# Attention with three full heads and a max-out layer: batches 2 and 3 loaded plainly and cast on the engines instead of by casting transfers

## The chip, the core and the metric

The kernel runs on one core of one Trainium2 chip. The metric is the device time of one execution in microseconds (us); lower is better.

## What is computed

```python
scores = q @ k^T / sqrt(64)                      # 4 batches, 8 heads, 768 x 64 each, f32
mask   = causal                                  # for "retrieval" heads (3 of the 8, by a flag array)
       = causal & (key < 4 or query - key < 64)  # for the other heads
a      = softmax(where(mask, scores, -1e9))
x      = (a @ v), heads side by side             # 3072 x 512
out    = maximum(x @ w1, x @ w2) @ w_out         # w1, w2: 512 x 1024; w_out: 1024 x 512
```

The kernel uses max(h1, h2) = relu(h1 - h2) + h2, so it multiplies x by w1 - w2, applies relu to get g, and adds x @ (w2 @ w_out) to g @ w_out. The product w2 @ w_out (`w2o` in the code) is made once.

## The kernel before

The work is cut into eight halves: four batches, each with two halves of 384 query rows. A half has two parts. *Attention* works on four pairs of heads. The heads are sorted at the start by the flags, so that the full heads come first. q and k are needed in bf16 and turned (head dimension on the partitions), v in bf16 as it lies. TensorE makes the scores (line 814), ScalarE the exponentials (833), VectorE applies masks (852) and divides by the sums (894, 904), and TensorE forms the weighted sums of v (877). The result x of a half is turned: by TensorE for batch 0 (1007), by a transposing transfer on SyncE for the others (1026). *Forward* is 32 up matmuls against w1 - w2 (1098), eight relus, and 36 down matmuls (1141) against w_out and w2o, then three copies to SBUF and three stores (1159).

How q, k and v come to bf16 differs by batch. For batches 0 and 1, `load_half` (492) loads f32 on SyncE's queue. The f32 tiles are cast by GpSimd, VectorE or ScalarE (`cast_qk`, `cast_v`), TensorE transposes q and k (`turn`, 655), and VectorE or ScalarE copies the turned tile out of PSUM (`unturn`). For batches 2 and 3, `load_pair` (522) issues casting transfers on GpSimd's queue (533), six for a pair, and one transposing transfer on SyncE's queue (546) turns q and k of a pair. A pair's destination is read from registers that hold the sorted heads.

There are three f32 buffers for loads (`NLD = 3`); A and B (the two halves of batch 0), w2, w1 and then the halves of the other batches take them in turn, and a load waits until the buffer's former tenant has been cast. w_out comes in four quarters as casting transfers on GpSimd's queue (`load_down`, 577, line 579). There are four output buffers (`NOUT = 4`).

The order of all instructions is fixed when the program is built. The class `Order` (`run`, 189) is a planner: each operation has a cost for each engine that can do it, the operations it depends on, and a rank, and the planner walks through planned time, giving each free engine its ready operation of lowest rank. TensorE has eight lists, searched in the order of `PE_LISTS`. Where the planner sees TensorE idle before `WARM_UNTIL`, it writes dummy matmuls on a tile of zeros (`warmer`, 457) into the program. What it writes is a fixed order on every engine, including the order of transfers on SyncE's and GpSimd's queues; on the chip each instruction then waits for its own semaphores, and everything behind it on its engine waits as well.

The lines that choose the way of a batch and the order of the first loads:

```python
LOADS = (
    'A', 'wo1', 'B', 'w22', 'w21', 'w12', 'w20', 'wo0', 'wo2', 'w10', 'masks', 'w11', 'w13',
    'w23', 'wo3',
)
LONG = ((0, 0), (0, 1), (1, 0), (1, 1))   # halves whose q and k come in one transfer, 768 B rows
CAST_BY_DMA = (2, 3)                      # batches that load_pair loads
...
        if b in CAST_BY_DMA:              # in prepare()
            if hf == 0:
                T["pair", n] = load_pair(b, p)
```

Of the kernel before, what the change touches and what calls it, by code (L numbers as in the profile page):

```python
# [12 lines left out]
BF16 = mybir.dt.bfloat16  # L13
I32 = mybir.dt.int32
ALU = mybir.AluOpType
ACT = mybir.ActivationFunctionType
# [119 lines left out]
class Order:  # L136
# [51 lines left out]

    def run(self, names, allowed):
        free = dict.fromkeys(("PE", "ACT", "DVE", "POOL", "SP"), 0.0)  # L190
        free["SP"], free["PE"] = 1.1, PE_BEGINS
        done_pe = []

        def used(t, span=3.4):
# [75 lines left out]
        while events:  # L270
            t = events[0][0]
# [79 lines left out]
        return max(o.end for o in self.ops)  # L351


WARM_UNTIL = 45.0
REGISTERS = 4.4
TURNED_BY_PE = (0,)
CAST_QK = {'POOL': 0.46, 'DVE': 0.27, 'ACT': 0.4}
CAST_V = {'POOL': 0.3, 'DVE': 0.26, 'ACT': 0.26}
RANK = {
    'cast': -1.1, 'vcast': -0.4, 'unturn': 1.2, 'mix_k': -2.6, 'mix_v': -1.1, 'exp': -1.35,  # L360
    'mask': 2.4, 'norm': -1.0, 'take_x': 1.05, 'turn': 1.9, 'w2b': 1.95, 'sub': -0.1, 'w2t':
    -0.75, 'wob': 0.5, 'w2o': -1.7, 'relu': -0.65, 'load': 0.7, 'out': 1.3, 'h2': -2.5,
}
NLD = 3
NQB = 4
# [4 lines left out]
NXT = 4  # L370
NG = 2
NOUT = 4
LONG = ((0, 0), (0, 1), (1, 0), (1, 1))
PE_LISTS = ('TX', 'W', 'S', 'TQ', 'P', 'H', 'P2', 'F')
PLACES = (0, 1, 2, 0, 1, 2, 0, 1, 2, 0, 1, 2)
SECOND_UP = False
LOADS = (
    'A', 'wo1', 'B', 'w22', 'w21', 'w12', 'w20', 'wo0', 'wo2', 'w10', 'masks', 'w11', 'w13',
    'w23', 'wo3',
)  # L380
BIAS = {'DVE': 2.5, 'ACT': 2.5}
BIAS_MIX = {}
W2B_BEHIND = True
NORM = {'DVE': 0.35}
TURNED_BY_DMA = ()
DMA_TURN = 0.19
PACE = 2
W2O_EARLY = 3
X_LAST = ((0, 0),)
BIASED = ((0, 0),)  # L390
DMA_BEGINS = 3.05
CAST_BY_DMA = (2, 3)
CAST_ISSUE = 0.85
CAST_RATE = 0.28
SPARE = {}
STEP = 2.0
FF_STEP = -1.1
S_AFTER = 2
PE_BEGINS = 1.3
COLD_UNTIL = 7.9  # L400
WARM_SHARE = 0.5
SHARE = {'S': 0.7, 'W': 0.9}
MARGIN = {'W': 0.3, 'S': 0, 'TQ': 0, 'F': 0.4}
X_MARGIN = 1.5


def tile_three_full_heads(
    tc, q, k, v, w1, w2, wo, out, tab, table_dram, heads, rez, found, verdict
):

    nc = tc.nc
# [30 lines left out]
    xts = keep.tile([128, NXT, NT, KC, 128], BF16, name="xt")  # L442
    gs = keep.tile([128, NG, FC, HALF], BF16, name="g")
    ots = keep.tile([128, NOUT, d_model], F32, name="ot")
    warm = keep.tile([128, 128], BF16, name="warmer")
    ones = keep.tile([128, 1], BF16, name="ones")
    banks = [psum.tile([128, 512], F32, name=f"ps{e}") for e in range(8)]
    nc.gpsimd.memset(warm, 0.0)  # L448
    nc.vector.memset(ones, 1.0)
    nc.gpsimd.memset(vbs[:, :, :, :, D:VW], 1.0)  # L450

# [70 lines left out]
    def load_pair(b, p):  # L522

        n = b * HP + p
        if p == 0:
            slot_of[b, 0], old, tenants[b] = slot()
            staged_old[b] = old
        got = {}
        for hh in range(2):
            for t, src in enumerate((q, k, v)):  # L530
                def emit(_, t=t, src=src, hh=hh):
                    to = vbs[:, n % NQK, hh, :, 0:D] if t == 2 else staged(n)[:, :, t, hh]
                    nc.gpsimd.dma_start(  # L533
                        out=to,
                        in_=src[b, bass.ds(heads[2 * p + hh], 1)].rearrange("o (i p) d -> p (o i) d", p=128),
                    )
                o = op(
                    {"POOL": CAST_ISSUE}, emit, [registers, *(last_w.get(n - NQK, ()) if t == 2 else ())],
                    data=0.197 / CAST_RATE, rank=RANK["load"], tag=f"load{b}.{p}", port=("POOL",),
                )  # L540
                if t < 2:
                    later.append((o, staged_old[b]))
                got[t, hh] = o

        def turn_pair(_):
            nc.sync.dma_start_transpose(
                out=qks[:, n % NQK].rearrange("f t (i c) -> f (t i) c", c=128),
                in_=staged(n).rearrange("p i t h d -> p (i t h d)"),
            )
        un = op(  # L550
            {"SP": 1.7}, turn_pair, [got[t, hh] for t in range(2) for hh in range(2)] + list(last_s.get(n - NQK, ())),
            data=DMA_TURN * 4 * NT, tag=f"turn{b}.{p}", rank=RANK["turn"],
        )
        tenants[b].append(un)
        return un, [got[2, 0], got[2, 1]]
# [21 lines left out]
    def load_down(c, behind):  # L577
        def emit(_):
            nc.gpsimd.dma_start(
                out=wob[:, 2 * c:2 * c + 2],  # L580
                in_=wo.rearrange("(c p) f -> p c f", p=128)[:, 2 * c:2 * c + 2],
            )
        return op({"POOL": 0.8}, emit, behind, data=2.097 / 4 / 0.36, rank=-1.0, tag=f"wo{c}")

    slot_of, tenants, bias_in, table_in, staged_old = {}, {}, [], [], {}
    w1_in, w2_in, wo_in, flow = {}, {}, {}, []
# [328 lines left out]
    def attend(b, hf):  # L915
# [81 lines left out]
        if b in TURNED_BY_PE:  # L997
            for c, tiles_ in enumerate(((0, 1), (2,))):
                key = ("px", b, hf, c)

                def emit(_, key=key, tiles_=tiles_):
                    px = bank(key, BF16)
                    x = xs[:, (2 * b + hf) % NX].rearrange("p i h d -> p i (h d)")
                    for e, i in enumerate(tiles_):
                        for kc in range(KC):
                            at = (e * KC + kc) * 128
                            nc.tensor.transpose(
                                px[:, at:at + 128], x[:, i, kc * 128:kc * 128 + 128], ident
                            )

                def take(e, key=key, tiles_=tiles_):
                    n = len(tiles_) * KC * 128
                    copy(
                        e, xts[:, (2 * b + hf) % NXT, tiles_[0]:tiles_[0] + len(tiles_)].rearrange("f i k c -> f (i k c)"),
                        bank(key, BF16)[:, 0:n],
                    )
                cols = len(tiles_) * KC * 128
                o = pe("TX", mm(*[128] * (len(tiles_) * KC)), emit, mine, claims=[(key, 1)])
                x_free.setdefault(len(x_free) if c == 0 else len(x_free) - 1, []).append(o)
                ready.append(op(  # L1020
                    {"DVE": 0.03 + cols / 1780, "ACT": act(cols)}, take, [o, *old],
                    frees=[key], rank=RANK["take_x"],
                ))
        else:
            def emit(_):
                nc.sync.dma_start_transpose(
                    out=xts[:, (2 * b + hf) % NXT].rearrange("f i k c -> f (i k) c"),
                    in_=xs[:, (2 * b + hf) % NX].rearrange("p i h d -> p (i h d)"),
                )
            o = op({"SP": 0.5}, emit, [*mine, *old], data=2.2, rank=-1.0)  # L1030
            x_free[len(x_free)] = [o]
            ready.append(o)
        x_ready[b, hf] = ready
# [347 lines left out]
def head_order(nc, small, is_retrieval, H):  # L1381

    raw = small.tile([1, 2 * H], I32, name="raw")
    nc.sync.dma_start(
        out=raw, in_=bass.AP(tensor=_as_int32(is_retrieval, 2 * H), offset=0, ap=[[0, 1], [1, 2 * H]])
    )
    number = small.tile([1, H], F32, name="number")
    for h in range(H):
        nc.vector.memset(number[:, h:h + 1], float(H - h))
    flag = small.tile([1, 2 * H], F32, name="flag")  # L1390
    r = small.tile([1, H], F32, name="r1")
    key = small.tile([1, H], F32, name="key")
    top = small.tile([1, H], F32, name="top")
    found = small.tile([1, H], F32, name="found")
    found_i = small.tile([1, H], I32, name="found_i")
    count = small.tile([1, 1], F32, name="count")
    vec = nc.vector
    vec.tensor_single_scalar(out=flag, in_=raw, scalar=0.0, op=ALU.not_equal)
    two = flag.rearrange("p (h two) -> p h two", two=2)
    vec.tensor_tensor(out=r, in0=two[:, :, 0], in1=two[:, :, 1], op=ALU.max)  # L1400
    vec.scalar_tensor_tensor(
        out=key, in0=r, scalar=2.0 * H, in1=number, op0=ALU.mult, op1=ALU.add
    )
    vec.max(out=top, in_=key)
    vec.tensor_scalar(
        out=key, in0=top, scalar1=2.0 * H, scalar2=-2.0 * H, op0=ALU.is_gt, op1=ALU.mult
    )
    vec.tensor_tensor(out=key, in0=key, in1=top, op=ALU.add)
    vec.tensor_scalar(
        out=found_i, in0=key, scalar1=-1.0, scalar2=float(H), op0=ALU.mult, op1=ALU.add  # L1410
    )
    vec.tensor_reduce(out=count, in_=r, op=ALU.add, axis=AX.X)
    return found_i, count
# [3 lines left out]
def kernel(  # L1417
# [38 lines left out]
    with tc.tile_pool(name="consts", bufs=1) as consts:  # L1456
        tab = consts.tile([128, table.shape[1]], BF16, name="tab")
        warm = consts.tile([128, 1], F32, name="warm")
        rez = consts.tile([128, B * H * S // 128], F32, name="rez")
        verdict = consts.tile([1, 1], I32, name="verdict")  # L1460
        found, count = head_order(nc, consts, is_retrieval, H)
        nc.scalar.dma_start(out=tab[:, 0:128], in_=table_dram.ap()[:, 0:128])
        nc.vector.memset(warm, 0.0)
# [4 lines left out]
        )  # L1468
        tile_three_full_heads(
            tc, q, k, v, moe_w1, moe_w2, moe_w_out, out, tab, table_dram, heads, rez, count,  # L1470
            verdict,
        )
        right = nc.values_load(
            verdict, min_val=0, max_val=1, skip_runtime_bounds_check_because="a product of two flags"
# [43 lines left out]
```

## Time and profile before

| | |
|---|---|
| three runs | 190.79, 192.16, 192.37 us (median 192.16) |
| profiled execution | 192.47 us, of which the profile's span is 190.8 us |
| busy of the span | TensorE 169.0, ScalarE 125.9, VectorE 87.8, GpSimd 58.7 us |
| moved | 32.10 MB in 89616 packets, 72946 of them under 512 bytes |
| mean granted TensorE clock | 0.974 |

The page gives busy times of one execution. PE is TensorE, PEld its weight loads, ACT ScalarE, DVE VectorE, POOL GpSimd, and SP SyncE, which only issues transfers; "SPq" and "POOLq" are issues of transfers. L1141 is line 1141 of the kernel. A group's row gives the count, then busy time and the mean time of one in ns, then the idle time just before and what ended it. In the rows of windows the columns are the stretch, its length, busy time and count of PE, PEld, DVE, ACT and POOL, the granted clock, the mean busy share of the transfer engines and GB/s. In a tile's row, three numbers with slashes are the shortest, the median and the longest in ns.

### The profile page before, as it was taken

How to read it: one execution, taken by the hardware profiler on the slowest of the kernel's cores; microseconds unless marked ns; L12 is line 12 of the kernel's file. 1: busy time of each engine (PE TensorE's matmuls, PEld its weight loads, DVE VectorE, ACT ScalarE, POOL GpSimd, SP SyncE). 2: the span in 40 equal slices, each digit the busy share in tenths (PEclk: the TensorE clock that was granted, in tenths of full speed). 3: DMA queues.
4: the chain of work that ended last, by engine and by line, in shares of the span. 5: the costliest groups of instructions: out<-in, count | busy, mean ns of one | idle time of the engine just before them, and what ended most of it. 6: DMA issues, size and time to landing. Idle time of an engine off the chain costs nothing.

```text
span 190.8 us, 4666 instructions
## 1 busy us (share of the span) xinstructions
PE 169.0 (89%) x1690; PEld 101.2 (53%) x1710; DVE 87.8 (46%) x261; ACT 125.9 (66%) x259; POOL 58.7 (31%) x98
## 2 busy tenths in 40 slices
PE   0999868996699999999999999699999999999960
PEld 0975638564346575566556655356466545445420
DVE  3165987975126668364243663785438500000000
ACT  3179894875448999999866974796978426417220
POOL 1100530357795829965475152000000000000000
PEclk9999985999999999999999999999999999999996
DMA  4999899999999979999999999993411322021121
GB/s 116 348 230 321 211 364 274 372 268 219 185 274 206 133 67 291 164 190 167 187 157 127 213 183 149 149 220 92 123 73 58 75 94 79 5 110 55 53 81 44
DMA packets 89616, 32.10 MB, mean 168 GB/s; under 512 B 72946, under 2 KB 86386, under 8 KB 89586
## 3 DMA queue, kind: packets, MB, share of 16 engines
q1 hardware_dynamic: 50722, 25.92, 59.3%
q0 software_dynamic: 38720, 5.77, 45.2%
q8 instruction: 15, 0.25, 0.5%
q14 instruction: 15, 0.12, 0.2%
q10 hardware_dynamic: 144, 0.03, 0.1%
HBM read 25.69 MB, written 6.29 MB: 168 GB/s over the span
## 4 chain that ended last, share of the span: by engine, by line
PE 64%; DMA 21%; SPq 10%; issue 1%; DVE 0%; ACT 0%; ACTq 0%
PE ps L1141 28%; PE ps L1098 17%; DMA xt<-x 7%; SPq L510 6%; DMA qk<-ld 6%; PE ps L877 6%; PE ps L814 6%; DMA wob<-in_moe_w_out_dram 4%; DMA ld<-in_moe_w_dram 4%; PE ps L1077 4%; SPq L498 2%; PE ps L1059 2%; PE ps L655 1%; SPq L558 1%; SPq L571 1%
## 5 line engine op out<-in xcount | busy, mean ns | idle before, releaser
L833 ACT ACTIVATE at<-ps 128x512 bf16<-128x512 f32 (+2 forms) x134 | 65.1, 569 | 7.6 <-PE ps L814 5.1
L1141 PE MATMUL ps<-wob,g 128*128 128x512 bf16 x184 | 45.8, 379 | 0.6 <-issue 0.3
L1098 PE MATMUL ps<-xt,w 128*128 128x384 bf16 x256 | 45.8, 326 | 0.3 <-DMA xt<-x 0.3
L1122 ACT ACTIVATE g<-ps 128x384 bf16<-128x384 f32 x56 | 27.4, 496 | 7.7 <-PE ps L1098 7.1
L1098 PEld LDWEIGHTS <-w 128*128 128x128 bf16 x256 | 23.5, 98 | 15.3 <-DMA xt<-x 0.8
L852 DVE TENSOR_TENSOR at<-at,tab 128x1024 bf16<-128x1024 bf16 (+5 forms) x49 | 24.0, 513 | 8.1 <-ACT at L833 7.8
L466 ACT COPY ot<-ps 128x512 f32<-128x512 f32 x21 | 12.3, 588 | 22.8 <-PE ps L1141 22.6
L1141 PEld LDWEIGHTS <-g 128*128 128x128 bf16 x192 | 17.3, 98 | 18.6 <-issue 0.4
L877 PEld LDWEIGHTS <-at 128*128 128x128 bf16 x477 | 20.8, 100 | 11.5 <-DVE at L852 3.2
L877 PE MATMUL ps<-vb,at 128*128 128x65 bf16 x387 | 23.5, 198 | 2.3 <-DVE at L852 1.7
L1141 PE MATMUL ps<-w2o,xt 128*128 128x512 bf16 x88 | 24.3, 379 | 0.4
L904 DVE TENSOR_TENSOR x<-ps,rez 128x192 f32 x64 | 22.7, 355 | 1.8 <-DMA xt<-x 0.2
L814 PE MATMUL ps<-qk 64*128 64x128 bf16 (+1 forms) x322 | 20.9, 232 | 0.6 <-DVE xt L468 0.3
L533 POOL DMA_DIRECT2D vb<-in_v_dram x16 | 13.2, 838 | 21.1 <-issue 8.1
L814 PEld LDWEIGHTS <-qk 64*128 64x128 bf16 x322 | 12.3, 95 | 11.3 <-issue 8.6
L894 DVE RECIPROCAL rez<-ps 128x6 f32<-128x6 f32 x32 | 5.5, 188 | 21.2 <-PE ps L877 21.2
L533 POOL DMA_DIRECT2D ld<-in_q_dram x16 | 13.4, 840 | 5.4 <-DMA ld<-in_q_dram 4.1
L533 POOL DMA_DIRECT2D ld<-in_k_dram x16 | 13.4, 836 | 4.9 <-DMA vb<-in_v_dram 2.7
L1141 PEld LDWEIGHTS <-xt 128*128 128x128 bf16 x96 | 8.9, 98 | 9.6
L468 POOL CAST qb<-ld 128x384 bf16 x18 | 8.9, 538 | 16.3 <-DMA ld<-in_k_dram 16.3
L457 PE MATMUL ps<-warmer 128*128 128x128 bf16 x81 | 7.8, 279 | 5.4 <-POOL warmer L448 4.6
L466 ACT COPY vx<-vb 64x408 bf16<-64x408 bf16 (+5 forms) x19 | 8.3, 465 | 4.2 <-DMA vb<-in_v_dram 3.9
(62 smaller groups left out, 137.0 us busy)
## 6 DMA issues: line engine op xcount, KB each, us to landing
out_dram<-ot SPq DMA_DIRECT2D x24, 256.0 KB, 3.6
ld<-in_moe_w_dram SPq DMA_DIRECT2D x8, 512.0 KB, 9.4
ld<-in_q_dram SPq DMA_DIRECT2D x4, 768.0 KB, 9.8
ld<-in_k_dram SPq DMA_DIRECT2D x4, 768.0 KB, 11.9
ld<-in_v_dram SPq DMA_DIRECT2D x12, 256.0 KB, 8.1
vb<-in_v_dram POOLq DMA_DIRECT2D x16, 96.0 KB, 9.9
ld<-in_q_dram POOLq DMA_DIRECT2D x16, 96.0 KB, 11.7
ld<-in_k_dram POOLq DMA_DIRECT2D x16, 96.0 KB, 11.7
```

The lines of the kernel that those rows point to most:

```text
L466: nc.scalar.copy(out=out, in_=in_)
L468: eng[e].tensor_copy(out=out, in_=in_)
L510: nc.sync.dma_start(out=lds[:, s, t, :, i * D:i * D + D], in_=src[b, :, r0:r0 + 128, :].rearrange("h p d -> p h d"),)
L533: nc.gpsimd.dma_start(out=to, in_=src[b, bass.ds(heads[2 * p + hh], 1)].rearrange("o (i p) d -> p (o i) d", p=128),)
L814: nc.tensor.matmul(to.rearrange("p (i c) -> p i c", c=128), lhsT=lhsT, rhs=q_of(n, i, m)[rows], start=bk not in under, stop=True, skip_gro ...
L833: nc.scalar.activation(out=at[:, bk, 0:w], in_=bank(("ps", b, hf, t), part=bk)[:, 0:w], func=ACT.Exp, scale=scale,)
L852: eng[e].tensor_tensor(out=at, in0=at, in1=tbl, op=ALU.mult)
L877: nc.tensor.matmul(po[:, hh, i - NT * hf, :], lhsT=ats[:, T["at", b, hf, t] % NAT, bk, e * 128:(e + 1) * 128], rhs=rhs, start=first, stop= ...
L904: nc.vector.tensor_tensor(out=xs[:, (2 * b + hf) % NX, :, bass.ds(heads[2 * p + hh], 1), :], in0=po[:, hh, :, 0:D].unsqueeze(2), in1=z[:, ...
L1098: nc.tensor.matmul(bank(key)[:, 0:HALF], lhsT=w[:, kc, fc * 128:(fc + 1) * 128], rhs=xts[:, (2 * b + hf) % NXT, :, kc, :], start=(kc == 0) ...
L1122: nc.scalar.activation(out=g, in_=ph, func=ACT.Relu)
L1141: nc.tensor.matmul(bank(key), lhsT=lhsT, rhs=(w2o if kind == "x" else wob)[:, c, :], start=(e == 0), stop=(e == len(steps) - 1),)
```

## The change

All of batches 2 and 3 is treated as batches 0 and 1 are: f32 loads on SyncE's queue, casts on GpSimd, VectorE or ScalarE, transposes of q and k on TensorE, copies out of PSUM. No transposing transfer of q and k and no casting transfer of q, k or v is left; the four casting transfers of w_out are. The tile of zeros is cleared as GpSimd's first instruction, ahead of its wait for the heads' order, and the flags are loaded on ScalarE's queue instead of SyncE's. The planner's ranks, costs and shares are other numbers, so that the whole order is written anew, and q and k of batch 1's first half come in six transfers of 256-byte rows instead of two.

```diff
-WARM_UNTIL = 45.0
+WARM_UNTIL = 38.0
 RANK = {
-    'cast': -1.1, 'vcast': -0.4, 'unturn': 1.2, 'mix_k': -2.6, 'mix_v': -1.1, 'exp': -1.35,
...
+    'cast': 1.35, 'vcast': 3.25, 'unturn': 2.05, 'mix_k': -1.3, 'mix_v': -0.85, 'exp': -0.55,
...
-LONG = ((0, 0), (0, 1), (1, 0), (1, 1))
+LONG = ((0, 0), (0, 1), (1, 1), (2, 1))
 LOADS = (
-    'A', 'wo1', 'B', 'w22', 'w21', 'w12', 'w20', 'wo0', 'wo2', 'w10', 'masks', 'w11', 'w13',
-    'w23', 'wo3',
+    'A', 'B', 'w23', 'w11', 'wo1', 'w20', 'w10', 'wo3', 'masks', 'wo2', 'w22', 'wo0', 'w21',
+    'w12', 'w13',
 )
-BIAS = {'DVE': 2.5, 'ACT': 2.5}
+BIAS = {'DVE': 2.5, 'ACT': 0}
-DMA_TURN = 0.19
-PACE = 2
+DMA_TURN = 0.25
+PACE = 0
-CAST_BY_DMA = (2, 3)
+CAST_BY_DMA = ()
-STEP = 2.0
-FF_STEP = -1.1
-S_AFTER = 2
+STEP = 0.65
+FF_STEP = -3.2
+S_AFTER = 3
-WARM_SHARE = 0.5
-SHARE = {'S': 0.7, 'W': 0.9}
-MARGIN = {'W': 0.3, 'S': 0, 'TQ': 0, 'F': 0.4}
-X_MARGIN = 1.5
+WARM_SHARE = 0.9
+SHARE = {'S': 0.45, 'W': 0.8}
+MARGIN = {'W': 2.0, 'S': 0.3, 'TQ': 2.0, 'F': 0.1}
+X_MARGIN = 0.8
...
-        return op({"POOL": 0.8}, emit, behind, data=2.097 / 4 / 0.36, rank=-1.0, tag=f"wo{c}")
+        return op({"POOL": 0.8}, emit, behind, data=2.097 / 4 / 0.36, rank=-9.0, tag=f"wo{c}")
...
-            o = op({"SP": 0.5}, emit, [*mine, *old], data=2.2, rank=-1.0)
+            o = op({"SP": 0.5}, emit, [*mine, *old], data=DMA_TURN * NT * KC, rank=-1.0)
...
 def head_order(nc, small, is_retrieval, H):
     raw = small.tile([1, 2 * H], I32, name="raw")
-    nc.sync.dma_start(
+    nc.scalar.dma_start(
...
+        warmer = consts.tile([128, 128], BF16, name="warmer")
+        nc.gpsimd.memset(warmer, 0.0)
         found, count = head_order(nc, consts, is_retrieval, H)
```

In the changed program line numbers are one or two lower (the down matmuls are L1140, the transposes L654).

More of the change, by code (lines that the diff above doesn't have):

```diff
@@ L190, in run @@
         free = dict.fromkeys(("PE", "ACT", "DVE", "POOL", "SP"), 0.0)
-        free["SP"], free["PE"] = 1.1, PE_BEGINS
+        free["SP"], free["PE"] = 0.75, PE_BEGINS
         done_pe = []
@@ L359 @@
 RANK = {
-    'cast': -1.1, 'vcast': -0.4, 'unturn': 1.2, 'mix_k': -2.6, 'mix_v': -1.1, 'exp': -1.35,
-    'mask': 2.4, 'norm': -1.0, 'take_x': 1.05, 'turn': 1.9, 'w2b': 1.95, 'sub': -0.1, 'w2t':
-    -0.75, 'wob': 0.5, 'w2o': -1.7, 'relu': -0.65, 'load': 0.7, 'out': 1.3, 'h2': -2.5,
+    'cast': 1.35, 'vcast': 3.25, 'unturn': 2.05, 'mix_k': -1.3, 'mix_v': -0.85, 'exp': -0.55,
+    'mask': -0.05, 'norm': -2.85, 'take_x': -1.45, 'turn': 0.4, 'w2b': 0.5, 'sub': -1.7, 'w2t':
+    -0.3, 'wob': -0.9, 'w2o': -2.2, 'relu': -3.25, 'load': 3.4, 'out': 3.05, 'h2': -0.2,
 }
@@ L390 @@
 BIASED = ((0, 0),)
-DMA_BEGINS = 3.05
-CAST_BY_DMA = (2, 3)
+DMA_BEGINS = 2.7
+CAST_BY_DMA = ()
 CAST_ISSUE = 0.85
-CAST_RATE = 0.28
+CAST_RATE = 0.24
 SPARE = {}
-STEP = 2.0
-FF_STEP = -1.1
-S_AFTER = 2
-PE_BEGINS = 1.3
-COLD_UNTIL = 7.9
-WARM_SHARE = 0.5
-SHARE = {'S': 0.7, 'W': 0.9}
-MARGIN = {'W': 0.3, 'S': 0, 'TQ': 0, 'F': 0.4}
-X_MARGIN = 1.5
+STEP = 0.65
+FF_STEP = -3.2
+S_AFTER = 3
+PE_BEGINS = 1.0
+COLD_UNTIL = 7.5
+WARM_SHARE = 0.9
+SHARE = {'S': 0.45, 'W': 0.8}
+MARGIN = {'W': 2.0, 'S': 0.3, 'TQ': 2.0, 'F': 0.1}
+X_MARGIN = 0.8
 def tile_three_full_heads(
-    tc, q, k, v, w1, w2, wo, out, tab, table_dram, heads, rez, found, verdict
+    tc, q, k, v, w1, w2, wo, out, tab, table_dram, heads, rez, found, verdict, warm
 ):
@@ L444, in tile_three_full_heads @@
     ots = keep.tile([128, NOUT, d_model], F32, name="ot")
-    warm = keep.tile([128, 128], BF16, name="warmer")
     ones = keep.tile([128, 1], BF16, name="ones")
     banks = [psum.tile([128, 512], F32, name=f"ps{e}") for e in range(8)]
-    nc.gpsimd.memset(warm, 0.0)
     nc.vector.memset(ones, 1.0)
@@ L537, in load_pair @@
                 o = op(
-                    {"POOL": CAST_ISSUE}, emit, [registers, *(last_w.get(n - NQK, ()) if t == 2 else ())],
+                    {"POOL": CAST_ISSUE}, emit,
+                    [*last_w.get(n - NQK, ())] if t == 2 else [first_w[b - 2, 1, p], *wo_in.values()],
                     data=0.197 / CAST_RATE, rank=RANK["load"], tag=f"load{b}.{p}", port=("POOL",),
@@ L1470 @@
             tc, q, k, v, moe_w1, moe_w2, moe_w_out, out, tab, table_dram, heads, rez, count,
-            verdict,
+            verdict, warmer,
         )
```

## The prediction

> **What bounds the kernel now.** I read the page's busy table first, then the windows by stage, the chain that ended last, and last the order of the transfers on SyncE's queue.
>
> ```profile
> span 190.8 us, 4666 instructions
> PE 169.0 (89%) x1690; PEld 101.2 (53%) x1710; DVE 87.8 (46%) x261; ACT 125.9 (66%) x259; POOL 58.7 (31%) x98
> ```
>
> TensorE (PE) is busy for 89%; no other engine passes 66%. The stages differ, so I cut the span where real work begins on TensorE, at its first down-projection matmul (L1141) and at its last one (columns: length, busy time and count by engine, granted clock, DMA share, GB/s).
>
> ```profile
> 0.00:10.60 10.60, 6.01 (x62) 6.02 (x62) 2.92 (x23) 2.83 (x5) 1.59 (x7) 1.00 0.83 230
> 10.60:53.03 42.43, 34.93 (x428) 23.30 (x430) 28.98 (x69) 30.87 (x61) 16.51 (x27) 0.92 1.25 273
> 53.03:184.25 131.22, 128.06 (x1206) 71.91 (x1220) 55.88 (x169) 91.60 (x192) 40.57 (x65) 1.00 1.05 135
> 184.25:190.80 6.55, 0.00 (x0) 0.00 (x0) 0.00 (x0) 0.59 (x1) 0.00 (x0) 0.75 0.14 48
> ```
>
> So there is an opening (to 53.03) in which TensorE idles 7.5 us, a long second stage in which it idles only 3.2 of 131 us, and a tail of 6.55 us that no edit touches. In the second stage whatever TensorE gains or loses is the kernel's. In the opening the chain and the waits name data:
>
> ```profile
> 20.98 7.70 DMA ld<-in_moe_w_dram
> 41.06 8.24 DMA wob<-in_moe_w_out_dram
> 53.19 2.59 PE ps L1141 x12
> 55.78 0.67 PE ps L655 x12
> 111.50 12.87 DMA xt<-x
> 176.74 7.52 PE ps L1141 x34
> ```
>
> ```profile
> PE ps L1077 <- DMA wob<-in_moe_w_out_dram: 3.3, 1, 3.3
> ```
>
> The last quarter of w_out (wob) is issued on GpSimd (POOL) at 41.06, and TensorE waits 3.3 us for it. Twelve transposes take 0.67 us (0.056 each), 34 down matmuls 7.5 (0.22 each).
>
> **The change, part by part.** (1) *Casting loads go.* The page counts what GpSimd spends on issuing them, and these are the prices of the casts that come instead:
>
> ```profile
> L533 POOL DMA_DIRECT2D vb<-in_v_dram x16 | 13.2, 838 | 21.1 <-issue 8.1
> L533 POOL DMA_DIRECT2D ld<-in_q_dram x16 | 13.4, 840 | 5.4 <-DMA ld<-in_q_dram 4.1
> L533 POOL DMA_DIRECT2D ld<-in_k_dram x16 | 13.4, 836 | 4.9 <-DMA vb<-in_v_dram 2.7
> L468 POOL CAST qb<-ld x18: 497/504/651, 19.7 to 65.3; 128x384 bf16 x18
> L466 ACT CAST qb<-ld x7: 506/507/512, 8.6 to 20.8; 128x384 bf16 x7
> L466 ACT COPY qk<-ps 128x768 bf16<-128x768 bf16 x9 | 6.9, 804 | 1.3 <-PE ps L655 1.2
> ```
>
> By the order of the changed program ScalarE (ACT) gets 15 casts of q and k more, 13 of v and 8 evictions of turned q and k: 15 x 0.507 + 13 x 0.36 + 8 x 0.80 = 18.7 us, less 5 relus and 2 output copies that move to VectorE and some copies of mixed v, about 13 in all. GpSimd loses 40 us of issuing and gains 17 x 0.50 + 19 x 0.35 = 15 of casts; VectorE (DVE) gains 8 evictions, about 8 us. I cost all of it at nothing: TensorE covers it, since in the stretch where these casts fall ScalarE has room.
>
> ```profile
> 50.00:150.00 100.00, 81.03 (x173) 1.00 1.36 158
> ```
>
> ```profile
> 150.00:184.25 34.25, 34.08 (x173) 16.83 (x173) 1.55 (x8) 13.24 (x26) 0.00 (x0) 1.00 0.22 74
> ```
>
> 81 + 13 is 94 of 100 us. If that cover is too thin, the exponentials come late first; up to 13 us are then at stake, but TensorE's last 34 us (the second row) are down and up matmuls that need none of them, so a late attention costs only where the written order has TensorE wait. I take 0.
>
> (2) *TensorE gets 96 transposes more*, two per 128 rows and pair for batches 2 and 3: 96 x 0.056 = 5.4 us. The new order puts 18 of them ahead of the first down matmul, 78 behind it: +4.4 in the second stage. The Trainium skill speaks against this price: TensorE: Matmul & The Clock Gate, Back-to-back issue gap, gives 81 ns for a 128-column matmul with its weight load; by it the 78 would cost 6.3 and my sum would end 1.9 us later. The row above has 0.056 sustained over twelve, so the measurement decides.
>
> (3) *The opening.* SyncE's first row goes to ScalarE's queue, so every load starts 0.41 us earlier (1.29 less 0.88); ScalarE's own load of the identity is 0.34 later, and nothing needs it before 10.6.
>
> ```profile
> 0.88 0.35 SPq L1384 DMA_DIRECT2D raw<-in_is_retrieval_dram  x1
> 1.29 0.42 SPq L498 DMA_DIRECT2D ld<-in_q_dram  x1
> 4.33 0.20 POOL L448 MEMSET warmer<- 128x128 bf16 x1 [3.74 <-DVE warm L1463]
> ```
>
> The warming tile is cleared first, so dummy matmuls start some 3 us earlier; real work waits for q and k, so this is worth 0. All four quarters of w_out now stand on GpSimd behind the casts of batch 0's second v, which ran at 22.40:
>
> ```profile
> 22.40 1.51 POOL L468 CAST vb<-ld 128x192 bf16 x5 [1.51 <-DMA ld<-in_v_dram]
> 23.87 1.44 POOL L579 DMA_DIRECT2D wob<-in_moe_w_out_dram  x2
> 31.60 2.06 SPq L498 DMA_DIRECT2D ld<-in_q_dram  x1
> 41.70 1.22 DVE L1043 TENSOR_TENSOR w<-ld 128x1024 bf16<-128x1024 f32 x1
> ```
>
> Issued by 27 they land before 40 at the 8.2 us of the chain, so the 3.3 us wait goes. What is late next: before its first down matmul the new order has 18 transposes of batch 1's first half, so q and k of that half must have landed and been cast. Bytes up to there, by the shapes: batch 0 4.7 MB, w1 and w2 4.2, w_out 2.1, tables 0.5, q and k 1.6: 13.1 MB.
>
> ```profile
> 0.00:25.00 25.00, 18.47 (x252) 14.10 (x254) 13.77 (x55) 15.71 (x32) 5.42 (x16) 1.00 0.92 251
> 25.00:40.00 15.00, 12.77 (x153) 9.28 (x155) 11.28 (x25) 11.30 (x21) 1.96 (x3) 0.77 1.17 322
> 40.00:53.03 13.03, 9.71 (x83) 5.94 (x83) 6.86 (x15) 6.68 (x15) 10.72 (x16) 1.00 1.65 223
> ```
>
> By 40 us 6.3 + 4.8 = 11.1 MB have moved. The other 2.0 take 6.2 us at 322 GB/s or 9.0 at 223 (the stretch with casting loads), so landing is at 45.8 to 48.6 after the 0.41. I take 46.2, near the fast end, because the casting loads are what fills the slow stretch. Casts 1.2, 18 transposes 1.0: first down matmul at 48.4, bounds 46 and 51. Against 53.03: -4.6 (-7 to -2). TensorE itself could be there sooner. Its 34.93 busy us hold 1.55 of dummies and a stretch at half clock:
>
> ```profile
> 12.00:53.00 41.00, 1.55 (x19) 1.16 (x19) 0.92 1.25 272
> 27.40:34.30 6.90, 5.62 (x70) 4.88 (x68) 4.87 (x11) 3.51 (x7) 0.85 (x2) 0.52 1.14 298
> ```
>
> 5.62 x 0.48 = 2.7 us. So 34.9 - 1.55 - 2.7 + 1.0 = 31.7 us of work, done at 42 if nothing waited: data set the opening.
>
> (4) *Waits of the second stage.* Most lie where the transposing loads of x (xt) are slow:
>
> ```profile
> 110.00:130.00 20.00, 17.74 (x200) 9.81 (x202) 12.56 (x43) 14.59 (x33) 4.28 (x6) 1.00 1.68 186
> ```
>
> 2.3 us idle. There GpSimd's v loads and SyncE's transposing loads of q and k (8 x L546) crowd the same engines; both go. I take -2.3 (0 to -2.3). New waits: -0.9 (the rest goes too) to +6.7 (rival A); taken 0, for the reason in A.
>
> The sum: -4.6 + 4.4 - 2.3 = -2.5 us. The profiled execution took 192.47 us (190.8 span and 1.67 around it), 0.31 above the median of 192.16. So 190.0 by its own time, 189.7 beside the median. Likeliest: **189.7**.
>
> **The rivals.** *A, x waits behind loads (slower).* SyncE's queue is one line. Before, the first transposing load of x stood behind two halves of batch 1:
>
> ```profile
> 51.54 10.31 SPq L510 DMA_DIRECT2D ld<-in_v_dram  x3
> 68.58 0.99 SPq L1159 DMA_DIRECT2D out_dram<-ot  x2
> 74.92 2.14 SPq L1026 DMA_TRANSPOSE xt<-x  x1
> ```
>
> In the new order it stands behind all loads of batches 1 and 2, batch 3's first half and three stores: 11.5 + 5 x 2.36 + 0.8 = 24.1 MB. TensorE wants it after 72 down matmuls (15.6), 32 up (5.2), 102 transposes (5.7) and some 10 us of scores and weighted sums: 48.4 + 36.5 = 84.9. From 11.1 MB at 40 us that needs 290 GB/s. At 322 it is in time, at 250 it lands at 91.6 and TensorE stands 6.7 us: 196.4. For it: batches 2 and 3 come in rows of 256 bytes, and the v loads of 51.54 took 3.4 us each to issue; against: these were beside casting loads, and 290 lies between 251 and 322. It decides below 290 GB/s. *B, faster still.* If data come at 322 GB/s or more throughout, the first down matmul is at 46 and nothing waits later: -7 + 4.4 - 2.3 = -4.9: 187.3. For it: the 25 to 40 row. *C, the opening gives back nothing.* The new order writes 78 dummies into the opening instead of 19; at 1.55 / 19 = 0.08 us that is 6.4 us that TensorE must run whether it waits or not. If they stand ahead of ready work, the first down matmul is at 51 and, with the waits at 110 to 130 kept, the sum is -2 + 4.4 = +2.4; with half of these waits gone 193.4, with all 192.3. I price C at 192.5. *D, the clock.* At 27.4 it fell to 0.52 behind scattered idling and cost 2.7 us; after 3.3 us of idling it stood at 1.00:
>
> ```profile
> 46.00:48.00 2.00, 0.07 (x3) 0.00 (x0) 1.75 (x6) 0.36 (x1) 0.82 (x2) 1.00 1.78 190
> 50.00:52.00 2.00, 2.00 (x18) 1.18 (x17) 0.32 (x1) 1.98 (x5) 2.00 (x5) 1.00 1.79 178
> ```
>
> If the wait for batch 1's q and k is longer than that one, the same 2.7 us fall on the down matmuls: 192.4. The Trainium skill has this as a rule (same page, What's actually happening): an idle window of about 3.4 us halves the clock. The first row agrees, the second shows that 3.3 us can pass. That the change does not do what it says I leave out: in the new order GpSimd issues the four quarters of w_out and no other load.
>
> **How the numbers follow.** Likeliest 0.34, B 0.20, C 0.14, D 0.06, A 0.26. A measurement of this kernel can tell about 1% (1.9 us) from no change. Faster: the likeliest and B, 0.54. Same: C and D, 0.20. Slower: A, 0.26. The likeliest's own range, by the bounds of the opening (-2.4, +2.6) and of the old waits (+2.3), is 187 to 194. Down to B and 2 us below, up to just short of A's price: 185.0 to 196.0, which leaves out the worse half of A and little else.
>
> **What would show it.** Right: first L1141 work (L1140 in the new program) at 46 to 51 us, no wait for wob, no clock near 0.5 in the opening; 78 transposes and 4.4 us more in the second stage; TensorE idle there under 3 us; ScalarE near 137 us. Wrong: a wait of the up matmuls for xt near 85 us (A); first down matmul at 51 or later (C), a clock of 0.5 around it (D); or ScalarE late, seen as TensorE's waits for exponentials above 3 us.

## The result, and the profile after

The changed kernel takes 199.76 us (median of four runs, 198.92 to 199.87); the kernel before took 192.26 us beside it (190.79 to 193.10). The ratio is 1.036, 95% interval 1.030 to 1.042: about 7 us slower, where 2.5 us faster was forecast. The profiled execution took 199.87 us. Ratios leave out disturbed runs, so they can differ a little from the quotient of two medians.

The busy row of the page after, and its windows cut at the same two events as before (first and last down matmul, now L1140; columns as before):

```profile
span 198.1 us, 5002 instructions
...
PE 176.8 (89%) x1851; PEld 110.1 (56%) x1873; DVE 101.3 (51%) x285; ACT 132.1 (67%) x277; POOL 37.3 (19%) x88
```

```profile
0.00:9.02 9.02, 6.33 (x71) 6.16 (x71) 2.05 (x21) 2.06 (x4) 0.83 (x6) 1.00 0.83 244
9.02:55.34 46.32, 37.95 (x500) 27.18 (x505) 28.34 (x71) 32.87 (x65) 10.74 (x25) 0.93 1.02 268
55.34:191.60 136.26, 132.50 (x1284) 76.76 (x1299) 70.91 (x196) 96.58 (x209) 25.70 (x57) 1.00 0.54 138
191.60:198.10 6.50, 0.00 (x0) 0.00 (x0) 0.00 (x0) 0.59 (x1) 0.00 (x0) 0.64 0.14 49
```

The spans differ by 7.3 us, in two parts. The opening ends 2.31 us later (55.34 against 53.03): real work begins 1.58 us earlier, but TensorE then idles 8.37 us instead of 7.50 (+0.87) and is busy 37.95 us instead of 34.93 (+3.02). The second stage is 5.04 us longer: 4.44 of busy TensorE, 0.60 of idle time. The tail is the same.

TensorE's waits after, by what released them (total, times, longest), and the pieces of its timeline around the longest one (start, length, what it was, and in brackets the idle time ahead of it):

```profile
PE ps L1058 <- DVE w2b L466: 5.7, 2, 4.5
PE ps L654 <- POOL qb L466: 1.8, 1, 1.8
PE ps L1097 <- DMA xt<-x: 1.7, 1, 1.7
PE ps L654 <- ACT qb L464: 1.7, 1, 1.7
```

```profile
29.32 0.28 PE L455 MATMUL ps<-warmer 128*128 128x128 bf16 x2
34.08 2.74 PE L1058 MATMUL ps<-tab,w2b 128*128 128x128 bf16 x24 [4.47 <-DVE w2b L466]
36.61 1.38 PE L455 MATMUL ps<-warmer 128*128 128x128 bf16 x11
...
54.34 1.17 PE L654 MATMUL ps<-tab,qb 128*128 128x128 bf16 x18
55.34 0.81 PE L1140 MATMUL ps<-wob,g 128*128 128x512 bf16 x3
```

The wait for wob is gone, as forecast. In its place stands a wait for the second quarter of w2, the last one to be loaded and cast, which the forecast does not name. 24 transposes of w2 stand in one block behind it and everything else behind them. Windows of after around it, and the rest of the opening:

```profile
30.00:32.00 2.00, 0.00 (x0) 0.00 (x0) 0.47 (x1) 0.00 (x0) 0.00 (x0) 1.00 1.18 251
34.00:36.00 2.00, 1.93 (x19) 1.93 (x20) 1.80 (x8) 0.00 (x0) 0.00 (x0) 0.50 1.16 257
36.00:38.00 2.00, 2.00 (x21) 1.80 (x21) 1.40 (x2) 2.00 (x3) 0.00 (x0) 0.50 1.09 375
38.00:40.00 2.00, 1.78 (x15) 1.05 (x17) 1.84 (x4) 2.00 (x5) 0.00 (x0) 0.53 1.18 333
40.00:55.34 15.34, 15.23 (x155) 9.55 (x156) 8.27 (x18) 10.64 (x24) 3.39 (x9) 1.00 0.95 248
```

TensorE stands still, then runs at half clock for six microseconds, and from 40 us to the first down matmul is busy 15.23 of 15.34 us. The 18 transposes of batch 1 (54.34) wait for nothing. So after 34 us it was not data that set the end of the opening but work.

Who makes w2 late: the issues of w_out on GpSimd, and the casts of the four quarters of w2 on VectorE in after; then the last of these casts in before.

```profile
22.94 0.83 POOL L578 DMA_DIRECT2D wob<-in_moe_w_out_dram  x1
24.36 2.14 POOL L578 DMA_DIRECT2D wob<-in_moe_w_out_dram  x3
```

```profile
24.88 0.69 DVE L466 CAST w2b<-ld 128x1024 bf16<-128x1024 f32 x1
26.19 0.83 DVE L466 CAST w2b<-ld 128x1024 bf16<-128x1024 f32 x1 [0.61 <-DMA ld<-in_moe_w_dram]
29.18 0.69 DVE L466 CAST w2b<-ld 128x1024 bf16<-128x1024 f32 x1 [1.70 <-DMA ld<-in_moe_w_dram]
33.32 0.69 DVE L466 CAST w2b<-ld 128x1024 bf16<-128x1024 f32 x1 [2.85 <-DMA ld<-in_moe_w_dram]
```

```profile
29.45 1.89 PE L1059 MATMUL ps<-tab,w2b 128*128 128x128 bf16 x16 [1.28 <-DVE w2b L468]
32.79 1.04 PE L1059 MATMUL ps<-tab,w2b 128*128 128x128 bf16 x8
36.08 0.61 PE L1059 MATMUL ps<-tab,w2b 128*128 128x128 bf16 x8
```

The last fence is TensorE before: there the quarter that came last is turned at 36.08, behind other work, and nobody waits for it. After, all four quarters of w_out are issued between 23 and 26.5 us, and TensorE's list wants the last quarter of w2 at 29.6.

### The profile page after: what moved, and what is told of

It reads as the page before. It is cut to its first block, busy times and chain, and to the rows that moved or that the text cites. A ratio compares the mean times of both kernels' runs of the same rounds, so it can differ in the third digit from the quotient of the medians.

```text
span 198.1 us, 5002 instructions
## 1 busy us (share of the span) xinstructions
PE 176.8 (89%) x1851; PEld 110.1 (56%) x1873; DVE 101.3 (51%) x285; ACT 132.1 (67%) x277; POOL 37.3 (19%) x88
## 5 line engine op out<-in xcount | busy, mean ns | idle before, releaser
L1140 PE MATMUL ps<-wob,g 128*128 128x512 bf16 x185 | 45.5, 379 | 0.5 <-issue 0.3
L1121 ACT ACTIVATE g<-ps 128x384 bf16<-128x384 f32 x51 | 25.1, 493 | 9.3 <-PE ps L1097 8.8
L851 DVE TENSOR_TENSOR at<-at,tab 128x1024 bf16<-128x1024 bf16 (+5 forms) x49 | 25.9, 536 | 8.7 <-ACT at L832 7.8
L466 POOL CAST qb<-ld 128x384 bf16 x35 | 17.7, 550 | 59.7 <-DMA ld<-in_k_dram 51.9
L1140 PEld LDWEIGHTS <-g 128*128 128x128 bf16 x192 | 17.2, 98 | 17.9 <-issue 0.4
L464 ACT COPY ot<-ps 128x512 f32<-128x512 f32 x19 | 11.2, 589 | 23.9 <-PE ps L1140 21.5
L1140 PE MATMUL ps<-w2o,xt 128*128 128x512 bf16 x85 | 23.4, 379 | 0.6
L876 PE MATMUL ps<-vb,at 128*128 128x65 bf16 x387 | 22.2, 193 | 0.0
L654 PE MATMUL ps<-tab,qb 128*128 128x128 bf16 x192 | 14.0, 219 | 4.0 <-POOL qb L466 1.8
L464 ACT CAST qb<-ld 128x384 bf16 x22 | 10.4, 541 | 7.2 <-DMA ld<-in_k_dram 6.3
L466 POOL CAST vb<-ld 128x192 bf16 x40 | 14.4, 403 | 3.2 <-DMA ld<-in_v_dram 3.1
L654 PEld LDWEIGHTS <-qb 128*128 128x128 bf16 x192 | 11.5, 98 | 5.8 <-POOL qb L466 2.0
L455 PE MATMUL ps<-warmer 128*128 128x128 bf16 x148 | 13.4, 254 | 1.0 <-POOL warmer L1461 1.0
L1140 PEld LDWEIGHTS <-xt 128*128 128x128 bf16 x96 | 8.9, 98 | 9.3
```

Of the source, the lines that this page charges most:

```text
L455: nc.tensor.matmul(banks[e][:, 0:128], lhsT=warm, rhs=warm, start=True, stop=True)
L464: nc.scalar.copy(out=out, in_=in_)
L466: eng[e].tensor_copy(out=out, in_=in_)
L654: nc.tensor.transpose(pt[:, t * HALF + i * 128:t * HALF + i * 128 + 128], qbs[:, T["qb", n, hf] % NQB, t, i].rearrange("p h d -> p (h d)") ...
L851: eng[e].tensor_tensor(out=at, in0=at, in1=tbl, op=ALU.mult)
L876: nc.tensor.matmul(po[:, hh, i - NT * hf, :], lhsT=ats[:, T["at", b, hf, t] % NAT, bk, e * 128:(e + 1) * 128], rhs=rhs, start=first, stop= ...
```

## The experiments

In all of them the opening ends at the first down matmul and the second stage 6.5 us before the end of the span; times beside each other come from one chip.

**Only the casting loads, with before's numbers.**

```diff
-CAST_BY_DMA = (2, 3)
+CAST_BY_DMA = ()
```

> The kernel before with CAST_BY_DMA = () and nothing else, so that its own planner numbers write the order for engine casts. Theory 1 (the loss is in the opening's new order, not in the casts): TensorE gets 5.4 us more, the 3.3 us wait for w_out and about 2 us at 110 to 130 go: 190 to 194 us. Theory 2 (casts and transposes on the engines cost the time by themselves): 197 us or more, with TensorE waiting on ScalarE or GpSimd in the second stage.

198.61 us against 193.98, ratio 1.033 (1.017 to 1.049). Its opening and second stage, and its largest wait in the second stage:

```profile
9.28:49.76 40.48, 36.76 (x478) 24.54 (x476) 33.18 (x77) 31.37 (x65) 11.47 (x27) 0.96 1.06 299
49.76:189.40 139.64, 133.75 (x1273) 76.45 (x1269) 59.66 (x175) 96.89 (x195) 33.23 (x80) 0.99 0.53 137
```

```profile
PE ps L655 <- POOL qb L468: 5.7, 3, 2.7
```

The opening is 3.3 us shorter than before's, much as forecast: with no casting loads of batches 2 and 3 in GpSimd's line w_out is in time. The second stage is 8.4 us longer: 5.7 of busy TensorE (1.7 of them because before's record there lacks 16 matmuls, as the sixth experiment shows) and 2.7 of idle time. So treating batches 2 and 3 the new way is a loss of the same size without any of the new numbers, and here the loss lies in the second stage. It does not show that the casts' own time is the price: two of the three casts that TensorE waits for had themselves waited for k to land (GpSimd idle for 3.58 and 5.63 us before them).

**Only the head: warming tile and flags**, in before's order.

```diff
-    nc.gpsimd.memset(warm, 0.0)               # in the kernel's body
+        nc.gpsimd.memset(warmer, 0.0)         # GpSimd's first instruction
...
-    nc.sync.dma_start(                        # flags
+    nc.scalar.dma_start(
```

> The kernel before with the two edits at its head alone (flags on ScalarE's queue, warming tile cleared first); the written order stays that of before. Both theories: loads start 0.4 us earlier, so 0 to 0.5 us less than before, 191.7 to 192.3. If one of the two edits costs something (identity later, dummies earlier), above 193.

193.09 us against 193.98, ratio 1.006 (1.000 to 1.011). The opening runs from 8.49 to 51.35 us, so its end comes 1.7 us earlier, and the second stage takes 133.45 instead of 131.27. The gain is given back; the last experiment comes to that.

**w2 loaded in the order in which TensorE turns it.**

```diff
-    'A', 'B', 'w23', 'w11', 'wo1', 'w20', 'w10', 'wo3', 'masks', 'wo2', 'w22', 'wo0', 'w21',
+    'A', 'B', 'w20', 'w11', 'wo1', 'w21', 'w10', 'wo3', 'masks', 'wo2', 'w22', 'wo0', 'w23',
```

> The kernel after with the quarters of w2 loaded in the order in which TensorE turns them (0, 1, 2, 3 instead of 3, 0, 2, 1). Theory 1: the 4.5 us wait at 34 us and the half clock behind it go, up to 2.8 us more: 193 to 196. Theory 2: 199 to 200, since the opening is bound elsewhere. Theory 3 (the 78 dummies of the opening stand ahead of ready work): 198 to 200.

198.83 us, against before 1.037 (1.025 to 1.048): no gain that can be told from 199.76. The wait for w2 is still 4.4 us, because the fourth cast (at 35.71) now stands on VectorE behind a subtraction that waits for a quarter of w1. The order of w2's quarters alone is not the cause; something makes the weights late whichever comes last.

**Few dummies.**

```diff
-WARM_SHARE = 0.9
+WARM_SHARE = 0.5
```

> The kernel after with WARM_SHARE = 0.5 as before: 13 dummies behind the first transposes instead of 78, the order of the rest nearly the same. Theory 3: 7.1 us of dummies become 1.1, so 194 to 196. Theory 1: they fill waits for data, so 198.5 to 200.5, and a clock that falls earlier may add up to 2.

198.69 us, 1.027 (1.013 to 1.041). 13 dummies instead of 78 take 3.28 us of busy time out of the opening (34.67 against 37.95; 0.05 each), its end comes 2.6 us earlier, but waits grow from 8.4 to 9.8 us there and the second stage is 2.4 us longer. So waits take back 1.4 of the 3.3 us in the opening, and the rest is lost in the second stage; the time can't be told from 1.036.

**Each transpose of batches 2 and 3 made twice.**

```diff
-                    nc.tensor.transpose(
+                    for _again in range(2 if n // HP >= 2 else 1):
+                        nc.tensor.transpose(
```

> The kernel after, each transpose of q and k of batches 2 and 3 made twice into the same place (96 more matmuls on TensorE, the written order unchanged). If TensorE bounds the second stage and a transpose costs 0.056 us there: 5.4 us more than after, 204.5 to 205.5, the second stage 141 to 142.5 us. If the casts or transfers bound it (waits in front of the transposes), the extra ones hide: 199 to 202.

203.67 us, 1.053 (1.041 to 1.065) where the changed kernel has 1.036: 3 to 4 us more, a little under the 204.5 that was expected. Its second stage:

```profile
53.41:195.00 141.59, 138.88 (x1398) 82.12 (x1395) 69.87 (x196) 97.02 (x209) 24.90 (x57) 1.00 0.54 139
```

The run without w_out, below, has the changed order with all 1302 matmuls recorded there: 134.16 us. 96 more take 4.7 (0.049 each), and most of it comes out in the time. In the second stage a transpose costs about what it takes.

**Before, with the fourth quarter of w_out issued with the second and third.** The order of all else is kept.

```diff
+            mine = [e for e in (c, 3) if e not in issued] if len(done) == 3 else [c]
+            for e in mine:                    # each quarter once
...
                 nc.gpsimd.dma_start(
```

> The kernel before with the last quarter of w_out issued together with the second and third, ahead of the casting loads of v; every other instruction stays in its order. If the 3.3 us wait is a loss of its own: the first down matmul at 49.5 to 50.5 instead of 53.0, and 188 to 190 in all. If the bytes only move the wait to w1, w2 or to the second stage: 191 to 193.

193.32 us against 193.76, 1.002 (0.993 to 1.010). Opening and second stage of its profile:

```profile
10.40:48.84 38.44, 35.21 (x430) 23.55 (x428) 28.41 (x67) 29.82 (x58) 14.14 (x22) 0.91 1.21 278
48.84:183.30 134.46, 129.74 (x1222) 72.06 (x1220) 57.74 (x171) 92.79 (x196) 43.59 (x70) 1.00 1.04 139
```

Without the wait for wob the opening ends 4.2 us earlier, and the second stage ends only 1.0 us earlier. The row shows something else: this order has 1222 matmuls in the second stage, and before's profile recorded 1206. Where a record is missing, the window seems to count a gap: of before's 3.2 us of idle time the waits that the profile names are 2.3. After's 1284 are 18 short of 1302 in the same way (3.8 us of idle time, 2.4 of named waits).

**The casting loads back, with after's numbers.**

```diff
-CAST_BY_DMA = ()
+CAST_BY_DMA = (2, 3)
```

> The kernel after with CAST_BY_DMA = (2, 3) again, all its other numbers kept. If the casts and transposes on the engines cost 4 to 5 us in the second stage: the second stage 131 to 133 and 194 to 196 in all, the opening still ending at 53 to 56. If the loss lies in the new numbers alone: 198 to 201.

210.71 us, 1.088 (1.074 to 1.101). In its profile (an execution of 211.9 us) the second stage took 151.39 us, with 15 us of named waits of TensorE, most of them for normalisation, masks and relus (5.6 us for x, 4.9 for masked exponentials). After's ranks and shares do not fit casting loads, so this says nothing of what the casting loads cost; the other way round, the first experiment is the fair one.

**After without w_out.** The four quarters are zeros written by GpSimd instead of loads; the output then lacks the product with w_out.

```diff
-            nc.gpsimd.dma_start(
-                out=wob[:, 2 * c:2 * c + 2],
-                in_=wo.rearrange("(c p) f -> p c f", p=128)[:, 2 * c:2 * c + 2],
-            )
+            nc.gpsimd.memset(wob[:, 2 * c:2 * c + 2], 0.0)
```

> The kernel after without loading w_out: its four quarters are filled with zeros by GpSimd, so 2.1 MB are not moved and the output lacks the weights. The written order of TensorE stays. If the four quarters together hold up w2 between 25 and 35 us: the last cast of w2 at 28 to 30 instead of 33.3, the 4.5 us wait and the half clock behind it gone, the first down matmul at 48 to 51, and 193 to 196 in all. If the opening is bound elsewhere: 198 to 200.

193.98 us against 193.76, 1.001 (0.997 to 1.006).

```profile
8.52:49.04 40.52, 35.97 (x504) 25.16 (x505) 31.21 (x71) 32.75 (x65) 12.43 (x25) 1.00 1.02 287
49.04:186.50 137.46, 134.16 (x1302) 76.86 (x1299) 70.36 (x196) 96.51 (x209) 24.95 (x57) 1.00 0.54 136
```

The last cast of w2 moves from 33.32 to 29.41, the clock stays at 1.00, and the opening ends at 49.04, six microseconds sooner. So the loads of w_out hold up w2. (The zeros are not free either: GpSimd writes three quarters of them at 23.33 to 26.06, and in that time a copy on VectorE takes 2.42 us that takes 0.25 in the changed kernel; the first cast of w2 starts at 26.53 instead of 24.88.) Even with w_out for nothing, though, the changed order is no faster than before.

**After with w_out behind w2.** GpSimd issues one quarter as before and the other three behind a one-column copy that reads the last quarter of w2; every engine's order is kept.

```diff
+            held.append(c)
+            if len(held) == 2:
+                at = 1 * (d_ff // 4)
+                nc.gpsimd.tensor_copy(out=seen[:, 0:1], in_=T["w2f"][:, KC - 1, at:at + 1])
             nc.gpsimd.dma_start(
```

> After, with the order of every engine kept, except that GpSimd issues only one quarter of w_out early and the other three behind a one-column copy that reads the last-loaded quarter of w2, so behind w2's landing. Theory 1 (the three quarters of w_out that share the transfer engines from 24 us are what makes w2 late, and nothing else is short): w2's last cast falls from 33.3 to about 30, TensorE's wait for w2b from 4.5 to about 2, the half-clock stretch behind it goes, the first down matmul comes at 50 to 51 and the time at about 195. Theory 2 (the bytes are what is short, whichever comes first): w2 is earlier but w_out, wanted by its first matmul at about 33 to 34 once TensorE no longer waits for w2, lands near 39; a wait for wob of 3 to 5 us takes the place of the wait for w2b, and the time stays at 198 to 200.

198.55 us against 194.06, ratio 1.023 (1.016 to 1.029). Its opening and second stage, the stretch in question, and the same stretch of the changed kernel:

```profile
8.58:49.81 41.23, 36.32 (x505) 25.01 (x506) 28.15 (x71) 32.50 (x63) 9.92 (x21) 1.00 1.04 272
49.81:189.30 139.49, 134.90 (x1302) 77.12 (x1299) 69.25 (x196) 96.98 (x210) 25.87 (x62) 1.00 0.56 144
...
24.00:34.00 10.00, 7.03 (x121) 5.64 (x120) 7.36 (x18) 6.80 (x12) 2.80 (x4) 1.00 1.11 346
```

```profile
24.00:34.00 10.00, 4.35 (x80) 3.31 (x77) 4.76 (x11) 5.31 (x11) 2.50 (x5) 0.95 1.14 286
```

For the opening theory 1 is right: the wait for w2 falls from 4.5 to 2.1 us, no half clock follows, w_out is not waited for, and the first down matmul comes at 49.81, earlier than expected. It was the order of the bytes and not their number: the two rows have 346 and 286 GB/s, but these count a casting load at half its f32 size (last section). Counted in f32, 3.7 MB come in the ten microseconds in both. For the time theory 1 is wrong: of the 5.5 us won in the opening the profile keeps 2.3, and the ratio falls from 1.036 to 1.023. The other 3.2 us go in the second stage. The waits named there rise from 2.4 to 3.7 us: 1.9 for xt, where the changed kernel has 1.7, and as a new one 1.3 for an eviction of g ahead of transposes. What takes the remaining 1.9 us the profile does not place.

**After, with q and k of batches 2 and 3 turned by transposing transfers.**

```diff
-TURNED_BY_DMA = ()
+TURNED_BY_DMA = (2, 3)
```

> After, with q and k of batches 2 and 3 loaded plainly and cast by the engines as in after, but turned by transposing transfers on SyncE's queue: TensorE has 96 matmuls fewer, ScalarE and VectorE 16 copies out of PSUM fewer. Theory 1 (TensorE bounds the second stage, so the transposes cost what they take): the second stage has about 4.3 us less of busy TensorE and its idle time stays near 2 to 4 us; with the opening near 53 to 55 the time is about 195. Theory 2 (transfers on SyncE's queue set it: 32 transposing transfers stand in one line with the loads and the transposing loads of x): TensorE gets waits for xt or qk of 4 us and more, and the time is 198 to 204.

201.89 us, 1.043 (1.036 to 1.050). TensorE's work falls (131.07 us busy for 1206 matmuls in the second stage), yet the time rises:

```profile
PE ps L813 <- DMA qk<-qb: 4.7, 1, 4.7
```

SyncE's queue has the transposing transfers in one line with loads and stores. One late transfer costs TensorE as much as the transposes of theory 1 were worth; theory 2 is right.

**Before, with batch 1 turned by transposing transfers**, 48 transposes fewer.

```diff
-TURNED_BY_DMA = ()
+TURNED_BY_DMA = (1,)
```

> Before, with q and k of batch 1 turned by transposing transfers instead of TensorE: the opposite of the change, 48 transposes fewer on TensorE. Theory 1 (TensorE bounds the second stage, each transpose costs its 0.054 us): up to 2.6 us less of busy time in the second stage, time 190.5 to 192. Theory 2 (the end of the second stage is set by what the transfers bring, since shorter openings were given back in waits): busy time falls but idle time rises by as much, and the time is 193 to 196.

221.42 us, 1.139 (1.134 to 1.144), far worse than both theories:

```profile
PE ps L877 <- DVE at L852: 18.6, 6, 7.9
PE ps L814 <- DMA qk<-qb: 9.4, 1, 9.4
```

The transposing transfers of batch 1 take 9.4 us from issue to landing (median), where those of the preceding experiment take 2.7. What makes the masked exponentials late was not traced, and the planner wrote a new order for this run, so the loss need not be the transfers' alone. In neither of these two runs were fewer transposes on TensorE to be had for less than they cost.

**Before, with the head and the early w_out.** Both parts of the opening that the forecast counted on, without the change of loads; the edits are those of the second and sixth experiments.

> Before with its order kept, the warming tile cleared first and the flags on ScalarE's queue, and the fourth quarter of w_out issued with the second and third: the two parts of the opening that the forecast counted on, without the transposes. By the forecast's sum (opening worth 4.6 us, nothing given back) 189. By theory 2 (a shorter opening is given back in waits of the second stage, as the profile of the early w_out alone showed: opening 4.2 us shorter, end only 1.0 us earlier) 192 to 193.5.

192.94 us against 194.06, ratio 0.988 (0.982 to 0.993): 1.2% faster than before by the ratio, 0.6% by the two medians, and inside theory 2's range. Its opening and second stage:

```profile
8.52:47.60 39.08, 35.38 (x428) 23.41 (x429) 28.73 (x71) 30.38 (x60) 14.10 (x22) 0.91 1.23 280
47.60:184.90 137.30, 131.91 (x1222) 73.45 (x1220) 57.83 (x171) 93.43 (x196) 43.27 (x70) 0.98 1.03 137
```

And one place where before's order takes the gain back, from the timeline and a window of the second experiment (head alone); here the same wait is 2.8 us. This run has a second such place: at 64.71 TensorE has waited 2.1 us for GpSimd's cast of q and k, which had itself waited for k to land, and the clock is 0.50 at 66 to 68.

```profile
116.61 1.04 PE L1139 MATMUL ps<-w2o,xt 128*128 128x512 bf16 x4
120.68 0.20 PE L875 MATMUL ps<-vb,at 128*128 128x65 bf16 x1 [3.03 <-DVE at L850]
...
120.93 1.64 PE L1139 MATMUL ps<-wob,g 128*128 128x512 bf16 x4
```

```profile
122.00:124.00 2.00, 2.00 (x27) 1.30 (x26) 1.74 (x6) 1.90 (x5) 0.41 (x1) 0.50 1.48 181
```

In before's order the first down matmul came at 53.03, 51.35, 48.84 and 47.60 us in the four profiles, and the last one ended at 184.3, 184.8, 183.3 and 184.9. In these four profiles an opening that is up to 5.4 us shorter brings an end at most 1.0 us earlier: TensorE waits for masked exponentials at 117 to 121 us (1.6 us before, 3.0 with the head alone and 2.8 here, these two with a half clock behind it). That the ratio is 1.2% under 1 all the same shows how little single profiles settle at that size.

## Why the prediction was wrong

**The opening (-4.6 forecast, +2.3 measured): the step that failed is "what is late next".** The wob wait went, as said, and w_out was issued by 27. But the forecast looked for the next deadline among the loads of batch 1 and took 46.2 us for their landing. (k had landed by 48.37, when the cast that GpSimd holds for it starts, and TensorE's transposes of it did not wait.) The late ones were already w2's quarters. It priced the earlier issue of w_out by what it brings, not by what it takes: 2.1 MB that share the transfer engines with w2 at 23 to 34 us. The experiment that puts w_out behind w2 gives that part back: the first down matmul comes at 49.81, inside the forecast's 46 to 51. "Data set the opening" failed too: TensorE had 15.23 us of work in the last 15.34. That k came within the forecast's 45.8 to 48.6 was luck: its 13.1 MB take w_out at 2.1 MB, the 11.1 MB of its rows take it at half (last section), so too much was left for after 40 us; and what came between 40 and 48.37 came at 199 GB/s, under both of its rates.

**The clock (rival D, 2.7 us).** The forecast's own trace had a half clock at 27.4 to 34.3, and the sum of TensorE's work let it go. It came back at 34 to 40, behind the wait for w2 and not around batch 1, where D had put it: 1.93 + 2.00 + 1.78 us of busy time at 0.50 to 0.53, of which some 2.8 us are lost by D's way of reckoning.

**The dummies (rival C).** C charged 78 of them 6.4 us. Without 65 of them the opening has 3.28 us less of busy time, 0.05 each, so 78 are 3.9 us; waits take back 1.4 of the 3.3, the second stage is 2.4 us longer, and the ratio of 1.027 (1.013 to 1.041) can't be told from 1.036. C's size was too large; how much of the rest is price and how much cover is not shown.

**The transposes (+4.4).** Right: 78 more, 4.44 us more busy time. Doubling them costs 4.7 us for 96, and the time rises by 3 to 4. The Trainium skill's 81 ns for a 128-column matmul with its weight load (TensorE: Matmul & The Clock Gate, Back-to-back issue gap) does not hold in these runs: 0.057 does, and 0.049 for the doubled ones.

**The waits of the second stage (-2.3 forecast, +0.6 measured): a mis-sized term.** The stretch at 110 to 130 is clean after the change, as forecast (the row is the changed kernel's):

```profile
110.00:130.00 20.00, 19.73 (x242) 11.66 (x243) 11.48 (x30) 16.01 (x36) 0.00 (x0) 1.00 0.29 81
```

But a wait of 1.7 us for xt stands at 94. Two errors: part of the 2.3 us seems to have been gaps of matmuls that the trace had not recorded (the one large wait there was 1.6 us), and the forecast took no wait to follow. The waits that the profile names in the second stage add up to 2.3 us before and 2.4 after.

**Casts at nothing.** Right for this order: ScalarE is busy 132.1 us (137 forecast: it took on 6 us and not 11), and none of TensorE's named waits of the second stage is for an exponential or a cast. In before's own order for the same casts (first experiment) TensorE does wait 5.7 us for them.

**Rival A** had the sign and the mechanism, at a quarter of its price. The transfers brought 252 GB/s between 40 and 88 us, under A's 290, and x was 1.7 us late instead of 6.7, because TensorE itself came to it at 92.5 us and not at 84.9. That A's 196.4 lies nearer to the result than the forecast is luck: the time was lost in other terms. When TensorE came 2.5 us sooner (w_out behind w2), x came 2.3 us sooner and was 1.9 us late: that line of loads is one of the places where a better opening is lost.

The whole account: of the 7.3 us between the two profiles the transposes hold 4.4, in the second stage, where nothing hides them; the late w2 with its half clock and the added dummies hold the opening's 2.3; the other 0.6 is idle time of the second stage, of which the named waits explain 0.1. With the opening mended (w_out behind w2) its end comes 3.2 us sooner than before's, and the ratio is still 1.023, since the second stage is then 8.2 us longer than before's: 4.4 of transposes, 1.4 of named waits (3.7 against 2.3), and 2.4 that the profiles do not place. The opening's gain is to be had without the transposes, and is then worth 1.2% by the ratio. Why the second stage of either order gives back most of a shorter opening is shown in its places (x and g after, the masked exponentials and a cast of q and k before) but not traced to one resource. A version of the changed order with the transposing loads of x ahead of batch 3's loads was not tried.

## What to carry to other kernels

When a transfer is moved earlier, list what it will share the transfer engines with and when TensorE's written order wants that, before looking at the next deadline. Where one engine is busy for 97% of a stage, its added work costs nearly in full, while time won ahead of that stage is won only as far as the stage's own latest input comes earlier as well. Compare the counts of matmuls before calling the rest of a window idle time, and ask at which size a rate counts a casting load.

## What was not expected of the hardware

The profile counts a casting load by the bf16 bytes that it writes, not by the f32 bytes that it reads. w_out is 2.1 MB in f32; the page of the changed kernel has its four quarters, and the queue that carries nothing else, at half of that:

```profile
wob<-in_moe_w_out_dram POOLq DMA_DIRECT2D x4, 256.0 KB, 9.8
q0 software_dynamic: 1088, 1.05, 3.1%
```

So a low GB/s beside casting loads is not by itself a loss of speed. At 24 to 34 us the changed kernel's queues moved 2.03 MB of plain and 0.81 MB of casting loads (286 GB/s), and with w_out behind w2 3.17 and 0.27 MB (346 GB/s). With the casting loads taken twice these are 3.65 and 3.71 MB; without w_out it was 3.48 MB, none of it by casting loads.

The length of a wait alone did not decide on the clock. After 3.03 us of idle time four down matmuls took 1.64 us instead of 1.04, at a granted clock of 0.50 (last two fences of the experiments); after 4.47 us it stood at 0.50 too, and after 2.1 us, with w_out behind w2, at 1.00. In the last experiment 2.1 us of waiting, with 0.3 more close behind, were followed by 0.50. But the 3.3 us at 46 to 49 in the kernel before, which the prediction shows, left it at 1.00. The Trainium skill (TensorE: Matmul & The Clock Gate, What's actually happening) puts the fall behind an idle window of about 3.4 us; a wait of 3.0 that had it and one of 3.3 that had not say that the wait is no measure of that window.
